# A memory-augmented recurrent transformer block: attention masks by multiplication, an earlier start, and a feed-forward part scheduled into the same ordered program

## The chip, the cores and the metric

One core of a Trainium2 chip runs the whole program. The metric is device time in microseconds (us), median of several runs. The core has five engines that run side by side, each in the order of its own instruction stream: TensorE (PE, matrix products from SBUF into PSUM), VectorE (DVE), ScalarE (ACT), GpSimd (POOL) and SyncE (SP, here only a queue of DMA issues). DMAs are issued from SP, ACT and POOL.

## The reference

The input x has 2048 tokens of width 640. It is normalised (layernorm without scale and shift) and cut into 64 segments of 32 tokens. Each segment is put behind a memory of 8 rows, attention runs over these 40 rows with 32 heads of width 128, and the first 8 rows of the projected output are the next segment's memory; the other 32 are the segment's result. So the 64 segments form a chain that can't be run in parallel. Then a feed-forward part (FFN) with a squared ReLU, 640 to 1728 to 640, is added to the residual.

```python
mask = (idx[:, None] < M) | (idx[:, None] >= idx[None, :])
for s in range(n_seg):
    h = jnp.concatenate([mem, xs], axis=1)
    q, k, v = (jnp.einsum('btd,dhe->bhte', h, W) for W in (Wq, Wk, Wv))
    scores = jnp.where(mask, jnp.einsum('bhqe,bhke->bhqk', q, k) * scale, -1e9)
    o = jnp.einsum('bhte,hed->btd', jnp.einsum('bhqk,bhke->bhqe', _softmax(scores), v), Wo)
    mem, out_s = o[:, :M], o[:, M:]
h = x + attention(layernorm(x))
h2 = h + relu(layernorm(h) @ w1 + b1)**2 @ w2 + b2
```

Memory queries see all 40 rows; a token sees the memory and the tokens up to itself.

## The kernel before, in words

**Blocks and steps.** 128 tokens are a block, four segments; there are 16 blocks (b) and 64 steps (b, sp). A step takes 32 rows through the chain: 8 memory rows and the first 24 tokens of the segment. The last 8 tokens of the four segments of a block are a tail of 32 rows, whose q, k and v are computed once a block by `tail_pass_fill`, and whose output projection by `wo_tail_fill`. These are cut into units and put in the list `fill`; `run_fill` (L228) pops some of them at places in a step where PE would wait. 32 rows fill a quarter of the PE array, so four groups of heads stand side by side (G = 4), in partitions 32g to 32g+31.

**Order.** A hand-written order holds on PE, ACT, DVE and POOL within the attention part (`manual_schedule`, L142): each of these runs its instructions as the program text emits them. SP's issues are placed by the framework. The FFN lies behind it, in pools of its own.

**A step** (`main_step`, L320): q in two halves, each 20 matmuls of 512 columns into a PSUM tile of tag mm (two buffers), copied out by ACT and DVE (`half`, `evac`); then the previous step's token values (`token_values`, L299: for each head index four matmuls with the step's values and four with the tail's); then k, v and transposes of q and k. The scores pss (L348) begin with two matmuls of the identity with mask tiles, which write 0 or -30000, and 64 matmuls of keys and queries add to them. ACT takes exp in three pieces: p for the memory queries, pk_s and p_lz for the token queries. p is spread over the groups (pbd), summed (pz), inverted and broadcast through PE (rz, rd, pb, rs), and gives the memory rows' values po, which are scaled into oT. For the token queries the sums are pzk (L406), their inverses rk, spread by POOL into rb. The output projection pw (`wo_pass`, L288) is 128 matmuls; in its middle `norm` (L421) turns rb by PE into pr and DVE makes pnk and pnl, the weights for the next step's token values. Then o is copied out by DVE, stored to DRAM (o_main), and `mem_to_hT` (L275) turns its 8 memory rows into hT, which the next step's q waits for.

**Layernorm** (L105): statistics on DVE, the inverse root on POOL as eleven or so small instructions (L117 to L127), the normalisation on DVE. Block b+1's statistics run at the start of block b, its normalisation and its five transposes (`ln_transpose`) at the start of the second step. x tiles have one buffer, and the next one's load is issued on SP.

**Start.** x of block 0, the memory, then Wq, Wk, Wv (for each, four slices of 128 partitions and 1 MB, and four of 32 partitions and 256 KB) and Wo (four of 1.25 MB) are issued, alternating between SP and ACT. x of block 1 comes after them. All three tail passes of block 0 run before the first step.

**FFN** (L474): when the attention's pools are released, w1, w2, b1 and b2 are loaded. Four tiles of 512 tokens: for each of four blocks the rows of o and x are loaded (main and tail rows apart, so that a block takes 13 DMAs), added, normalised, transposed into hnT; hb is the residual plus b2 (POOL, L518). Then 14 groups of 5 matmuls (psf, L525), each followed by ReLU on ACT and a square on DVE (f1T, one buffer), and for each block two groups of 14 matmuls (psy, L538), whose result plus hb is yo, stored by 8 DMAs per block.

Of the kernel before, what the change touches and what calls it, by code (L numbers as in the profile page):

```python
# [9 lines left out]
ALU = mybir.AluOpType  # L10
AX = mybir.AxisListType
F32 = mybir.dt.float32
# [5 lines left out]
def kernel(  # L18
# [16 lines left out]
    nc = tc.nc  # L35
# [21 lines left out]
    NEG = -30000.0  # L57
# [23 lines left out]
    for g in range(G):  # L81
# [3 lines left out]
    nc.vector.memset(mask_m[0:32], 0.0)  # L85
    nc.gpsimd.affine_select(out=mask_m[0:32], in_=mask_m[0:32], compare_op=ALU.is_ge,
                            fill=NEG, base=M, pattern=[[0, HG], [1, HD]], channel_multiplier=-1)
    mask_t = const.tile([128, 4, HG, M + TL], BF16)
    nc.vector.memset(mask_t[0:32], 0.0)
    for sp in range(4):  # L90
        mt = mask_t[0:32, sp]
        nc.gpsimd.affine_select(out=mt, in_=mt, compare_op=ALU.is_ge, fill=NEG, base=-TL * sp,
                                pattern=[[0, HG], [0, M + TL]], channel_multiplier=1)
        nc.gpsimd.affine_select(out=mt, in_=mt, compare_op=ALU.is_ge, fill=NEG, base=TL * sp + TL - 1,
                                pattern=[[0, HG], [0, M + TL]], channel_multiplier=-1)
        mtt = mask_t[0:32, sp, :, M:M + TL]
        nc.gpsimd.affine_select(out=mtt, in_=mtt, compare_op=ALU.is_ge, fill=NEG, base=TL * sp,
                                pattern=[[0, HG], [1, TL]], channel_multiplier=-1)
    for g in range(1, G):
        nc.gpsimd.dma_start(out=mask_m[32 * g:32 * g + 32], in_=mask_m[0:32])  # L100
        nc.gpsimd.dma_start(out=mask_t[32 * g:32 * g + 32], in_=mask_t[0:32])
    ones64 = const.tile([64, 128], BF16)
    nc.vector.memset(ones64[:], 1.0)

    def layernorm(pool, src, dst, strips=False):  # L105
        FMAX = nc.vector.BN_STATS_FMAX
        nsub = 1
        while D // nsub > FMAX or D % nsub:
            nsub += 1
        st = pool.tile([128, nsub, nc.vector.BN_STATS_DIM], F32, tag="lnst")  # L110
        xr = src.rearrange("p (s f) -> p s f", s=nsub)
        for s_ in range(nsub):
            nc.vector.bn_stats(out=st[:, s_, :], in_=xr[:, s_, :])
        mv = pool.tile([128, nc.vector.BN_AGGR_DIM], F32, tag="lnmv")
        nc.vector.bn_aggr(out=mv[:], in_=st[:])
        ve = pool.tile([128, 1], F32, tag="lnve")
        nc.gpsimd.tensor_scalar(out=ve[:], in0=mv[:, 1:2], scalar1=EPS, scalar2=None, op0=ALU.add)  # L117
# [462 lines left out]
```

## Time and profile before

| what | us |
|---|---|
| median of 5 runs (1438.25 to 1443.64) | 1442.44 |
| the profiled execution's own time | 1442.44 |
| its span, first to last instruction | 1440.7 |
| PE busy | 1233.6 (86%) |
| DVE busy | 508.8 (35%) |
| ACT busy | 465.8 (32%) |
| POOL busy | 194.2 (13%) |

The profile is one execution, recorded by the hardware. A row of its timeline gives the start, the duration, the engine (PE for matmuls, PEld for their weight loads, SPq and ACTq for issues of DMAs), the line of the kernel, the operation, output<-inputs with shapes, and the count; in brackets stands the idle time before it and what ended that. A group row gives the busy time of all, the mean ns of one, and the idle time before them. A row of the windows view gives, for a stretch, the busy time of PE, PEld, DVE, ACT and POOL, PE's granted clock, the DMA engines' busy share and GB/s. A row of the waits view gives the total, the number and the longest of a wait.

### The profile page before, as it was taken

What the parts mean: (1) busy time and instruction counts of PE and PEld (TensorE: products, weight loads), DVE (VectorE), ACT (ScalarE), POOL (GpSimd) and SP (SyncE); (2) the same over time, 40 slices, a digit from 0 to 9 for tenths busy, and PEclk for the clock granted to TensorE, in tenths of its full rate; (3) what the DMA queues carried; (4) which work ended last, traced back from release to release, by engine and by line L of the source; (5) the groups of instructions that cost most, each with busy time, mean ns of one, the idle gap of its engine ahead of it and who ended that gap; (6) DMA issues with size and microseconds to landing.
All of it is one profiled execution on the core that took longest, in us unless ns stands there. A gap on an engine that the chain in (4) does not pass through costs nothing.

```text
span 1440.7 us, 69707 instructions
## 1 busy us (share of the span) xinstructions
PE 1233.6 (86%) x32376; PEld 705.3 (49%) x32376; DVE 508.8 (35%) x1398; ACT 465.8 (32%) x1001; POOL 194.2 (13%) x684
## 2 busy tenths in 40 slices
PE   1399999999999999989999999998999998158888
PEld 0155555555555555555555555554555555024444
DVE  1033334333333333433333333333434333144442
ACT  0233333333333333333333333333333333022222
POOL 2001010101010100001010101010101000263420
PEclk9899999999999999999999999999999999569999
DMA  9800000000000000000000000000000000521200
GB/s 312 285 10 5 12 6 12 6 12 6 12 6 12 6 12 5 13 6 12 6 12 5 12 5 13 6 10 6 12 5 8 5 7 8 162 47 48 53 26 19
DMA packets 39396, 44.00 MB, mean 31 GB/s; under 512 B 24448, under 2 KB 36464, under 8 KB 37184
## 3 DMA queue, kind: packets, MB, share of 16 engines
q1 hardware_dynamic: 29440, 23.25, 5.8%
q10 hardware_dynamic: 9344, 15.98, 3.5%
q8 instruction: 253, 4.15, 1.2%
q0 software_dynamic: 320, 0.30, 0.1%
q14 instruction: 39, 0.32, 0.1%
HBM read 33.44 MB, written 5.94 MB: 27 GB/s over the span
## 4 chain that ended last, share of the span: by engine, by line
PE 77%; DMA 7%; DVE 5%; ACT 5%; issue 3%; POOL 1%; ACTq 0%; DVEq 0%; SPq 0%
PE ps L198 38%; PE pw L218 11%; PE pt L211 6%; PE psy L538 5%; PE psf L525 4%; PE ps L218 3%; ACT row L191 2%; DMA xt<-in_A_x_dram 2%; PE po L393 2%; DVE row L193 2%; PE po L304 1%; PE pss L361 1%; PE pss L357 1%; DMA wk<-in_A_Wk_dram 1%; DMA w<-in_B_w_dram 1%
## 5 line engine op out<-in xcount | busy, mean ns | idle before, releaser
L198 PEld LDWEIGHTS <-hT 128*32 128x32 bf16 x7680 | 179.7, 96 | 211.8 <-issue 54.7
L191 ACT CAST row<-ps 128x512 bf16<-128x512 f32 x192 | 112.8, 588 | 327.9 <-PE ps L198 313.4
L198 PE MATMUL ps<-wv,hT 128*32 128x512 bf16 x2560 | 177.3, 383 | 15.5 <-DVE vr L193 12.0
L218 PE MATMUL pw<-wo,oT 128*32 128x160 bf16 x8320 | 172.4, 234 | 17.7 <-issue 10.5
L198 PE MATMUL ps<-wk,hT 128*32 128x512 bf16 x2560 | 162.7, 383 | 16.8 <-DVE row L193 11.5
L218 PEld LDWEIGHTS <-oT 128*32 128x32 bf16 x8320 | 148.6, 97 | 40.8 <-issue 21.3
L198 PE MATMUL ps<-wq,hT 128*32 128x512 bf16 x2560 | 153.8, 382 | 14.4 <-ACT row L191 11.3
L193 DVE CAST row<-ps 128x512 bf16<-128x512 f32 x128 | 88.5, 692 | 211.2 <-PE ps L198 211.2
L211 PE MATMUL pt<-ident,row 128*128 128x128 bf16 x1280 | 113.4, 221 | 38.6 <-ACT row L191 26.2
L211 PEld LDWEIGHTS <-row 128*128 128x128 bf16 x1280 | 76.0, 98 | 129.5 <-issue 98.6
L416 POOL CAST rb<-rk 128x256 bf16<-128x256 f32 x64 | 25.8, 403 | 565.7 <-DVE rk L414 565.7
L191 ACT COPY kT<-pt 128x512 bf16<-128x512 bf16 x128 | 75.4, 589 | 17.4 <-PE pt L211 17.3
L380 DVE TENSOR_TENSOR pbd<-p,ones 128x256 bf16<-128x256 bf16 x128 | 48.7, 422 | 90.3 <-ACT p L364 90.3
L193 DVE CAST vr<-ps 128x512 bf16<-128x512 f32 x64 | 44.3, 692 | 101.5 <-PE ps L198 101.5
L525 PE MATMUL psf<-hnT,w 128*128 128x512 bf16 (+1 forms) x280 | 71.8, 419 | 9.5 <-ACT r L528 6.4
L314 POOL COPY oTt<-oT 128x256 bf16<-128x256 bf16 x64 | 25.8, 403 | 392.2 <-DVE oT L193 385.4
L191 ACT CAST oT<-po 128x256 bf16<-128x256 f32 x128 | 41.4, 376 | 92.4 <-PE po L308 91.0
L191 ACT COPY qT<-pt 128x512 bf16<-128x512 bf16 x64 | 37.6, 587 | 98.0 <-PE pt L211 98.0
L538 PE MATMUL psy<-w,f1T 128*128 128x320 bf16 x448 | 68.0, 300 | 0.3 <-DVE f1T L529 0.2
L426 DVE TENSOR_TENSOR pnk<-pk_s,pr 128x256 bf16<-128x256 bf16 x64 | 27.0, 421 | 116.1 <-PE pr L424 116.1
L404 DVE TENSOR_TENSOR oT<-po,rs 128x128 bf16<-128x128 f32 x128 | 31.3, 287 | 74.4 <-ACT rs L400 74.4
L198 PEld LDWEIGHTS <-hTt 128*32 128x32 bf16 x1920 | 41.8, 97 | 29.9 <-issue 9.8
(104 smaller groups left out, 1509.7 us busy)
## 6 DMA issues: line engine op xcount, KB each, us to landing
o_main<-o SPq DMA_DIRECT2D x65, 40.0 KB
xt<-in_A_x_dram SPq DMA_DIRECT2D x16, 160.0 KB
wo<-in_A_Wo_dram SPq DMA_DIRECT2D x2, 1280.0 KB
wo<-in_A_Wo_dram ACTq DMA_DIRECT2D x2, 1280.0 KB
w<-in_B_w_dram SPq DMA_DIRECT2D x1, 2160.0 KB
w<-in_B_w_dram ACTq DMA_DIRECT2D x1, 2080.0 KB
wq<-in_A_Wq_dram ACTq DMA_DIRECT2D x2, 1024.0 KB
wq<-in_A_Wq_dram SPq DMA_DIRECT2D x2, 1024.0 KB
```

The costliest lines, as they stand in the source:

```text
L191: nc.scalar.copy(out=out_, in_=in_)
L193: nc.vector.tensor_copy(out=out_, in_=in_)
L198: nc.tensor.matmul(ps[32 * g:32 * g + 32, :], lhsT=lhs(c), rhs=w[:, c, g * EG + n * 512:g * EG + (n + 1) * 512], start=(c == 0), stop=(c = ...
L211: nc.tensor.transpose(out=pt[:, k * 128:(k + 1) * 128], in_=row[:, i * 128:(i + 1) * 128], identity=ident[:])
L218: nc.tensor.matmul(ps[32 * g:32 * g + 32, 0:DG], lhsT=lhs(h), rhs=wo[:, h, g * DG:(g + 1) * DG], start=(h == 0), stop=(h == H - 1))
L314: nc.gpsimd.tensor_copy(out=oTt[:, :, sp * TL:(sp + 1) * TL], in_=oT[:, :, SEG:NQ])
L380: nc.vector.tensor_tensor(out=pbd[:, a], in0=p[:, a].unsqueeze(2).to_broadcast([128, HG, G, M]), in1=ones4[:].unsqueeze(1).unsqueeze(3).to ...
L393: nc.tensor.matmul(po[:, i * SEG:(i + 1) * SEG], lhsT=v[:, i * E:(i + 1) * E], rhs=pbd[:, a, i].rearrange("p g q -> p (g q)"), start=(a == ...
L404: nc.vector.tensor_tensor(out=oT[:, k * 16:(k + 1) * 16, 0:M].rearrange("p (g i) q -> p g i q", g=2), in0=pov[:, gs], in1=rs[:].rearrange( ...
L426: nc.vector.tensor_tensor(out=pnk[:], in0=pk_s[:], in1=pr[:, 0:NK], op=ALU.mult)
L525: nc.tensor.matmul(ps[0:fs, :], lhsT=w1[:, c, fc * 128:fc * 128 + fs], rhs=hnT[:, c, :], start=(c == 0), stop=(c == DC - 1))
L538: nc.tensor.matmul(ps[:, 0:320], lhsT=f1T[0:fs, fc, k * 128:(k + 1) * 128], rhs=w2[0:fs, fc, cs], start=(fc == 0), stop=(fc == FC - 1))
```

## The change: what it does

**Masks.** The mask matmuls go. The mask tiles now hold 1 and 0; POOL multiplies pk_s (its first 24 columns of each head) and p_lz by them after exp. For the memory queries' tail keys, a table ones4t (made once) takes the place of ones4. The first key-query matmuls start the PSUM tile.

**Token sums.** pzk, rk and rb move from behind pb into the middle of the output projection (`sums`), and pr, pnk and pnl from there behind it. The token-value matmuls are the same, all of the step's values first and then all of the tail's.

**Layernorm** is cut in three: first half of the statistics; second half and root; normalisation. For block b+2 these run in the middle of the projections of steps (b, 2), (b, 3) and (b+1, 0). x tiles have two buffers. The transposes stay at the second step of a block; the tail copy goes first.

**Start.** x of blocks 0 and 1 is loaded first and both layernorms run before the first step. The wide weight slices are all on SP, the narrow ones all on ACT, Wo on both. The tail passes of block 0 run inside the first step, each before the main pass of its weight.

**FFN** comes into the same ordered program and the same pools. w1 is loaded by five SP DMAs in the last step, into the slot of Wq; w2 by POOL's queue after the first tile's root. Its working tiles lie in the slots of Wk, Wv and Wo. The rows are loaded for whole tiles of four blocks (9 DMAs a block, in natural order), the next tile's ahead: its statistics run in the groups of psf, its root (one for four blocks) and hb on POOL after them, its normalisation and transposes between the groups of psy. f1T and hnT have two buffers, r has three, psy uses the four psum_v tiles, and yo is stored by one DMA per block.

```diff
-            nc.tensor.matmul(psv[:, :, M:SEG], lhsT=ident[:], rhs=mask_m[:], start=True, stop=False,
-                             skip_group_check=True)
-            nc.tensor.matmul(psv[:, :, NQ:NC], lhsT=ident[:], rhs=mask_t[:, sp], start=False, stop=False,
-                             skip_group_check=True)
...
+            pkh = pk_s[:].rearrange("p (i q) -> p i q", q=SEG)[:, :, 0:HD]
+            nc.gpsimd.tensor_tensor(out=pkh, in0=pkh, in1=mask_m[:], op=ALU.mult)
+            nc.gpsimd.tensor_tensor(out=p_lz[:, :, HD:SEG], in0=p_lz[:, :, HD:SEG], in1=mask_t[:, sp], op=ALU.mult)
...
-            def norm():
-                pr = psum_t.tile([128, 512], F32, tag="pt", name="pr")
+            def sums():
+                pzk = psum_t.tile([128, 512], F32, tag="pt", name="pzk")
...
+                for f in side.get((b, sp), ()):
+                    f()
+            o = wo_pass(b * 4 + sp, sums)
+            pr = psum_t.tile([128, 512], F32, tag="pt", name="pr")
...
+                if sp == 2 and b + 2 < NB:
+                    lns = ln_block(b + 2)
+                    side[b, 2], side[b, 3], side[b + 1, 0] = [lns[0]], [lns[1]], [lns[2]]
+                if b == NB - 1 and sp == 3:
+                    last = ffn_load
...
+        load_x(1)
...
-                (nc.sync if c % 2 else nc.scalar).dma_start(out=w[:, c, :], in_=w2d[c * DG:c * DG + 128, :])
+                nc.sync.dma_start(out=w[:, c, :], in_=w2d[c * DG:c * DG + 128, :])
             for g in range(G):
-                (nc.sync if g % 2 else nc.scalar).dma_start(out=w[32 * g:32 * g + DR, 4, :],
-                                                            in_=w2d[g * DG + 128:(g + 1) * DG, :])
+                nc.scalar.dma_start(out=w[32 * g:32 * g + DR, 4, :], in_=w2d[g * DG + 128:(g + 1) * DG, :])
```

The ends of attention and the FFN's loop:

```diff
+        loads(0)
+        token_values(*pend.pop())
...
+        for k in range(NK4):
+            stats(0, k)
+        root(0)
+        ffn_load2()
+        loads(1)
+        for k in range(NK4):
+            apply(0, k)
+            turn_f(0, k, "act" if k % 2 == 0 else "dve")
...
+                if nxt and fc in (2, 4, 6, 8):
+                    stats(t + 1, fc // 2 - 1)
+                if t == 0 and fc >= FC - NK4:
+                    hbias(nc.vector, 0, fc - FC + NK4)
+            if nxt:
+                root(t + 1)
+            if t + 2 < NTL:
+                loads(t + 2)
...
+                    if nxt and k in (1, 2):
+                        apply(t + 1, (k - 1) * 2 + hf)
+                    nc.vector.tensor_tensor(out=yo[:, cs], in0=ps[:, 0:320], in1=hbs[t % 2 * NK4 + k][:, cs], op=ALU.add)
+                    if nxt and k in (1, 2):
+                        turn_f(t + 1, (k - 1) * 2 + hf)
+                nc.sync.dma_start(out=out2d[b * 128:(b + 1) * 128, :], in_=yo)
```

`loads`, `stats`, `root`, `apply`, `turn_f` and `hbias` are new functions of the FFN: a tile's row loads, residual sum and statistics, inverse root, normalisation, transposes, and residual plus b2.

More of the change, by code (lines that the diff above doesn't have):

```diff
@@ L334, in main_step @@
                 token_values(*pend.pop())
+            if first:
+                fill.extend(first[1])
+                run_fill(100)
             half(wk, lhs, 0, kr, "act")
@@ L339, in main_step @@
             turn(kr, 0, kT[:, 0:4], "act")
+            if first:
+                fill.extend(first[2])
+                run_fill(100)
+            if last:
+                last()
             pv0 = psum.tile([128, 512], F32, tag="mm", name="ps")
```

332 lines of the change are left out of this document (191 added, 141 removed).

## The prediction, made before the change was run

> **What bounds the kernel now.** I read the page first: span, the slices, the chain that ended last.
>
> ```profile
> span 1440.7 us, 69707 instructions
> ...
> PE   1399999999999999989999999998999998158888
> ...
> PE 77%; DMA 7%; DVE 5%; ACT 5%; issue 3%; POOL 1%; ACTq 0%; DVEq 0%; SPq 0%
> ```
>
> Each digit is one fortieth of the span (36 us). TensorE (PE) is full in the middle, the 64 recurrent steps, and empty at two places: the first two slices (loading) and slices 34 and 35 (from attention to FFN). So there are three stages, with three limits. The profiled execution took 1442.44 us, which is also the median of the five runs; its span is 1440.7, so 1.7 us lie around the span. All sums below are on the span's clock.
>
> **Start.** The windows view gives DMA GB/s in its last column; the timeline gives start, duration, engine, line.
>
> ```profile
> 23.00:30.00 7.00, 1.14 (x12) 0.18 (x4) 0.00 (x0) 0.00 (x0) 0.00 (x0) 1.00 1.03 414
> 30.00:34.00 4.00, 0.00 (x0) 0.00 (x0) 0.00 (x0) 0.00 (x0) 0.00 (x0) 1.00 1.04 221
> 66.00:68.00 2.00, 0.00 (x0) 0.00 (x0) 0.00 (x0) 0.00 (x0) 0.00 (x0) 0.50 0.07 22
> ...
> 68.27 0.89 DVE L113 BATCH_NORM_STATS2 st<-xt 128x6 f32<-128x320 bf16 x2 [52.99 <-DMA xt<-in_A_x_dram]
> ...
> 70.00 2.33 PE L198 MATMUL ps<-wk,hT 128*32 128x512 bf16 x20 [8.28 <-DVE row L193]
> ...
> 73.23 1.42 PE L198 MATMUL ps<-wv,hT 128*32 128x512 bf16 x12
> ...
> 82.97 0.19 PE L277 MATMUL pm<-ident,o 128*128 128x32 bf16 x1 [0.43 <-DVE o L223]
> ```
>
> The weights have landed by 66 us (22 GB/s after it), and yet the first step hands its memory on (pm) at 82.97: VectorE (DVE), in program order, sat on the statistics of block 1, whose x was loaded last, so that PE waited 8.28 us for a copy queued behind them. The change loads both x blocks first and finishes both layernorms, which removes that 8.28 us wait; gives ACT the twelve 256 KB slices and half of Wo; and runs the q, k and v tail passes each when its own weight is there. What is late next are the transfers themselves, 21.5 MB before and after. Wide slices move at 414 GB/s, 32-partition slices at 221. Ahead of the last Wv slice lie 12.9 MB wide (31 us) and 3.15 MB narrow (14 us), with 2 us to start: 47 us; with ACT's 2.6 MB of Wo (wide) drawn ahead, 53. From Wv's arrival, the v tail pass (half of the 40-matmul rate above, 2.3 us) and then 82.97-73.23 = 9.7 us lead to pm: 59 to 65. But pm also needs all of Wo, landed at 66 as before, half a projection (1.3) and its copy (0.7): 68. I take 68: **15 us gained**. Bounds: with the transfers ending 6 us later because one queue carries more of them (no row shows that), 9; with narrow and wide slices mixing well and ending at 62, 19.
>
> **Loop.** A steady step with a tail pass as filler:
>
> ```profile
> 600.24 0.26 PE L350 MATMUL pss<-mask_m,ident 128*128 128x192 bf16 x1
> ...
> 600.48 0.37 PE L357 MATMUL pss<-qT,kTt 128*32 128x16 bf16 x32
> ...
> 602.10 0.39 ACT L370 ACTIVATE pk_s<-pss 128x256 bf16<-128x256 f32 x1
> ...
> 602.46 0.42 DVE L386 TENSOR_TENSOR rd<-ident,rz 64x256 bf16<-64x256 bf16 x1
> ...
> 603.23 0.18 PE L409 MATMUL pzk<-ones,pk_s 128*128 128x4 bf16 x1
> ...
> 603.41 1.05 PE L198 MATMUL ps<-wq,hTt 128*32 128x512 bf16 x16
> ...
> 605.94 0.28 PE L424 MATMUL pr<-ident,rb 128*128 128x128 bf16 x2
> 606.15 1.29 PE L218 MATMUL pw<-wo,oT 128*32 128x160 bf16 x64
> 606.26 0.42 DVE L426 TENSOR_TENSOR pnk<-pk_s,pr 128x256 bf16<-128x256 bf16 x1 [1.86 <-PE pr L424]
> 606.60 0.21 DVE L427 TENSOR_TENSOR pnl<-p_lz,pr 128x64 bf16<-128x64 bf16 x1
> ...
> 607.21 0.18 PEld L198 LDWEIGHTS <-hTt 128*32 128x32 bf16 x8
> ...
> 607.50 0.33 DVE L223 CAST o<-pw 128x160 bf16<-128x160 f32 x1 [0.68 <-PE pw L218]
> ...
> 608.24 0.20 DVE L281 CAST hT<-pm 128x40 bf16<-128x40 f32 x1 [0.42 <-PE pm L279]
> ...
> 608.49 2.34 PE L198 MATMUL ps<-wq,hT 128*32 128x512 bf16 x40
> ```
>
> PE works in order, so differences of neighbouring starts are what its groups cost. **Masks:** two matmuls go, 600.48-600.24 = 0.24 us, on a stretch where PE has no gap. **pzk** leaves the place ahead of the filler (603.41-603.23 = 0.18) for the middle of the output projection, where pr stood (606.15-605.94 = 0.21): 0.21 gained there and in the middle, of which pr is given back behind the projection. **The tail of the step:** call 607.21 T, the end of the projection. Before, o is copied by T+0.62, pm follows, hT is written from T+1.03 and q starts at T+1.28. After, pr (0.21) and two fill units stand ahead of pm, which moves to T+0.67 at the earliest, its result usable at about T+1.03; DVE must do o, then pnk and pnl (spacing 0.34, then 0.18) before hT: 0.62+0.34+0.18 = T+1.15. So q at T+1.40, 0.12 later. Net 0.24+0.18+0.03-0.12 = 0.33 us a step. **Layernorm:** the normalisation of the next block moves from right ahead of its transposes into an earlier projection:
>
> ```profile
> PE pt L180 <- DVE xn L136: 22.1, 16, 12.7
> ```
>
> Of the 22.1 us, 12.7 is the first block; (22.1-12.7)/15 = 0.63 a block goes. That step has a second o copy (0.33) now behind pnl, so I keep 0.35 of it. Per block 4 x 0.33 + 0.35 = 1.7; fifteen blocks and a last one without fillers (0.15 a step): **26 us gained**.
>
> The masks are now GpSimd (POOL) multiplications of 192 and 64 columns, which before doesn't show. The nearest rows:
>
> ```profile
> L518 POOL TENSOR_TENSOR hb<-ht,b2b 128x640 f32<-128x640 bf16 x16 | 22.6, 1415 | 60.9 <-DVE ht L508 60.9
> ...
> 1379.95 0.43 DVE L529 TENSOR_TENSOR f1T<-r 128x512 bf16<-128x512 bf16 x1 [0.65 <-ACT r L528]
> ...
> 1380.89 1.40 POOL L518 TENSOR_TENSOR hb<-ht,b2b 128x640 f32<-128x640 bf16 x1 [0.47 <-DVE ht L508]
> ...
> 1381.26 1.31 DVE L529 TENSOR_TENSOR f1T<-r 64x512 bf16<-64x512 bf16 x1
> ```
>
> At 1415/640 = 2.2 ns a column they take 0.43 + 0.15, from 602.55 (exp done at 602.49) to 603.2; pzk reads them at 605.5. The cover is 2.3 us: nothing on the path. Behind them on POOL wait only rb, which needs pzk anyway, and the copies into oTt and qT for the next step, several us from use; and on DVE nothing but hT waits behind pnk, which is counted above. Bounds: nothing, to the whole 0.6 a step if something else waits for POOL. That can happen: a DVE multiplication that takes 0.43 alone took 1.31 while POOL's 1.40 us one ran. rd (602.46) starts 0.09 ahead of POOL's first multiplication, so I expect POOL to wait and nothing to be lost; if POOL wins, rd is 0.4 late, pb behind it stalls PE by as much, and 64 steps give back 26 us. The Trainium skill ("SBUF — State Buffer", section "SBUF: two separate sides") says that the shared port pair is an exclusive lock, that whoever starts first has it for the whole instruction, and that DVE needs it when it has two SBUF inputs. The 1.31 us row agrees; by that rule the sum holds if rd's lead holds, and is the next rival if not.
>
> The reordered token-value matmuls are the same 64, and the DVE statistics in mid-projection (0.9 us at most, against a 1.29 us half) are covered; without cover each costs its length once a block.
>
> **FFN.**
>
> ```profile
> 1230.00 0.45 PE L218 MATMUL ps<-wo,oTt 128*32 128x160 bf16 x13 [1.62 <-issue]
> ...
> 1250.58 0.49 DVE L508 TENSOR_TENSOR ht<-ot,xt 128x640 bf16<-128x640 bf16 x1 [10.21 <-DMA xt<-in_A_x_dram]
> ...
> 1252.03 0.21 DVE L115 BATCH_NORM_AGGREGATE mv<-st 128x2 f32<-128x12 f32 x1
> ...
> 1256.45 0.45 DVE L136 TENSOR_SCALAR hn<-ht,mv,rstd 128x640 bf16<-128x640 bf16 x1 [4.22 <-POOL rstd L127]
> ...
> 1277.15 12.64 PE L525 MATMUL psf<-hnT,w 128*128 128x512 bf16 x45 [0.78 <-ACT hnT L515]
> ...
> 1398.83 0.45 PE L513 MATMUL pt<-ident,hn 128*128 128x128 bf16 x5 [0.69 <-DVE hn L136]
> ...
> 1402.13 17.07 PE L525 MATMUL psf<-hnT,w 128*128 128x512 bf16 x70 [0.78 <-ACT hnT L515]
> ...
> 1419.14 16.96 PE L538 MATMUL psy<-w,f1T 128*128 128x320 bf16 x112
> ...
> L499 SPq DMA_DIRECT2D ot<-o_main x64: 290/322/576, 1231.5 to 1363.3; - x64
> ```
>
> Before, 46.7 us pass between the last projection (1230.45) and the first FFN matmul (1277.15): weights and rows are only then loaded, and four layernorms run one after another, each with its 4.2 us of POOL. After, w1 and the rows of tile 0 are issued within the last step into freed weight slots. What is left: 1 us because pnk and pnl are now behind the last projection with nothing to cover them (1231.5), o's copy, four statistics of 1252.24-1250.58 = 1.66 us, one root for all four (4.2), then four normalisations, transposes and copies overlapping (about 5): 1231.9+6.6+4.2+5 = 1247.7. **29.5 us gained.** It hangs on tile 0's 36 row loads: SP issues one in 0.32 us (median, last row) to 0.58, so all in 12 to 21. They can start once the last Wv pass frees its slot, 607.21-600.48 = 6.7 us ahead of the end of a projection, and the two final projections take 256 matmuls at 64 in 1.3, with their pause 7 us: 14 of cover, and statistics that follow one block at a time. Just in time; without any cover some 16 us come on top.
>
> From there on before took 1440.7-1277.15 = 163.5 us, its first three tiles (1402.13-1277.15)/3 = 41.7 each, the last, with no layernorm beside it, 17.0+17.0 = 34.0. After, the next tile's layernorm and transposes stand within the tile: 34.0 x 4 plus 20 transposes (4 x 0.45) three times, 141.4, and an end of 4 (one store for eight): 145.4. **18 us gained.** DVE has 1.66 more in every second 1.08 us group, so it falls up to 2.5 us behind, which the three r buffers just hold. w2 (2.1 MB) comes on POOL's queue after the root, issued at 1243 and needed at 1264.5; its cost is nothing if it lands within 21 us. POOL's queue landed 160 KB in 6.7 us, and 0.1 KB in 7.5:
>
> ```profile
> b2b<-in_B_b_dram POOLq DMA_DIRECT2D x1, 160.0 KB, 6.7
> b1b<-in_B_b_dram POOLq DMA_DIRECT2D x1, 0.1 KB, 7.5
> ```
>
> So size does not show, and 7.5 plus 2.1 MB at 221 GB/s is 17. Bounded by 13 times the 160 KB row it would be 90, 70 too late; I take the first.
>
> **Sum:** 1440.7-15-26-29.5-18 = 1352.2, and 1.7 around it: **1354 us**.
>
> **The rivals.** (1) POOL wins the port and rd waits: the loop gives back 26 us, 1380. For it: only 0.09 us of lead. Against: rd needs only DVE's order, while POOL's start needs exp, whose end (602.49) lies behind rd's start. (2) A late transfer in the FFN: out stores queue on SP behind the 36 row loads of the tile after next (16 us), the two yo buffers stay full, DVE's normalisation waits, and PE stalls some 4 us in two tiles; or w2 lands late: 1362. (3) The loop yields the masks only (0.24 x 64 = 15) because the DVE tail is longer than read: 1365. (4) The change doesn't do what it says, the early loads wait for their slots until attention ends: the 29.5 us stay, 1383. (5) Slower: POOL's multiplications are so slow on their strided 192 columns that pzk waits. They have 2.9 us from 602.55 to 605.5; the gains outside are 88 us, 1.4 a step, so above 4.3 us, seven times my price, the kernel is slower; at 5 us, (5-2.9) x 64 = 134 is added: 1488. The 2.2 ns a column speaks against it. (6) Still faster, under 1337: transfers mix well and the steps lose further waits.
>
> **Numbers.** Forecast 0.55 (its own range 1337 to 1368, from the bounds of the start and 0.15 us a step either way), rival 1 0.14, rival 2 0.11, rival 3 0.08, rival 4 0.04, rival 5 0.02, rival 6 0.06. The range 1337 to 1381 leaves out rivals 4 to 6. About 0.3% (4.3 us) is what a measurement can tell from no change. Only rival 5 is not faster, and a mixture of several losses could end at no change: faster 0.96, same 0.02, slower 0.02.
>
> **What would show it.** The first pm near 68; starts of exp p in neighbouring steps 0.3 us closer; POOL's multiplication over before 603.5 in the step's clock and rd still 0.42 long; the first psf some 16 us after the last projection; tiles of 34 to 36 us with PE unbroken. Wrong if rd grows to 0.8, if PE waits for pzk, or if psy or the FFN transposes wait for a DMA.

## The result and the profile after

| what | before | after |
|---|---|---|
| median, us | 1442.66 (16 runs, 1438.25 to 1449.58) | 1347.52 (9 runs, 1344.43 to 1353.26) |
| ratio to before | | 0.9339, 95% interval 0.9322 to 0.9357 |
| span of the profiled execution | 1440.7 | 1345.9 |
| first step's pm | 82.97 | 71.86 |
| first pm to last pm | 1121.8 | 1095.0 |
| last pm to the end of the final projections | 25.7 | 24.2 |
| from there to the first psf | 46.7 | 18.3 |
| first psf to the end | 163.5 | 136.6 |

The kernel is 95 us faster. The forecast was 1354, 6.5 us above the measurement, inside its range. The five stages of the table gain 11.1 + 26.8 + 1.5 + 28.4 + 26.9 = 94.7 us of span; forecast were 15, 26, nothing, 29.5 and 18.

From the page of the changed kernel, the span, PE's slices and the shares of the chain that ended last:

```profile
span 1345.9 us, 69184 instructions
...
PE   1699989898989899999999999989898989849999
...
PE 82%; DVE 5%; DMA 5%; ACT 5%; issue 3%; SPq 1%; POOL 0%; ACTq 0%; DVEq 0%
```

The second slice went from 3 to 6, the hole of two slices between attention and FFN (1 and 5) is now one slice (4), and the last four slices are full. PE's share of the chain rose from 77% to 82%.

**The start**, PE's timeline of the changed kernel (start, duration, engine, line, operation; in brackets the idle time before it and what ended that):

```profile
56.20 0.40 PE L206 MATMUL ps<-wv,hTt 128*32 128x512 bf16 x4 [0.92 <-DMA wv<-in_A_Wv_dram]
59.23 3.18 PE L206 MATMUL ps<-wv,hTt 128*32 128x512 bf16 x28 [2.63 <-DMA wv<-in_A_Wv_dram]
...
68.72 1.29 PE L226 MATMUL pw<-wo,oT 128*32 128x160 bf16 x64 [0.79 <-DVE oT L438]
...
71.86 0.19 PE L285 MATMUL pm<-ident,o 128*128 128x32 bf16 x1 [0.22 <-DVE o L231]
```

The wait for a copy behind the second block's statistics is gone, and in its place PE waits for Wv's last slice. From 59.23 to pm it takes 12.6 us: 2.9 for the last 28 matmuls of the v tail pass, to 62.17, at a granted clock of 0.50 (windows view, 57.4 to 64.1), and 9.7 from there, as forecast.

**A step** of the changed kernel, the same place as in the prediction, all engines:

```profile
223.64 0.42 DVE L420 TENSOR_TENSOR rd<-ident,rz 64x256 bf16<-64x256 bf16 x1
...
223.75 0.72 POOL L404 TENSOR_TENSOR pk_s<-pk_s,mask_m 128x192 bf16<-128x192 bf16 x1 [6.12 <-ACT pk_s L400]
...
224.43 0.30 POOL L405 TENSOR_TENSOR p_lz<-p_lz,mask_t 128x64 bf16<-128x64 bf16 x1
...
226.94 0.18 PE L450 MATMUL pzk<-ones,pk_s 128*128 128x4 bf16 x1
...
228.34 0.29 PE L463 MATMUL pr<-ident,rb 128*128 128x128 bf16 x2
228.46 0.33 DVE L231 CAST o<-pw 128x160 bf16<-128x160 f32 x1 [0.95 <-PE pw L226]
...
229.47 0.20 DVE L289 CAST hT<-pm 128x40 bf16<-128x40 f32 x1 [0.18 <-PE pm L287]
```

rd starts 0.11 us ahead of POOL's multiplication and takes 0.42 us as before. The multiplications take 1.0 us, not the 0.58 of the forecast, and end at 224.73, 2.2 us before pzk reads them. Over all 64 steps rd takes 416 to 419 ns.

**The FFN**, PE's timeline of the changed kernel:

```profile
1209.31 16.24 PE L621 MATMUL psf<-fk,fw 128*128 128x512 bf16 x70 [0.68 <-DVE b1f L613]
1225.48 6.40 PE L642 MATMUL psy<-fw,fk 128*128 128x320 bf16 x42
1231.81 0.45 PE L591 MATMUL pt<-ident,fw 128*128 128x128 bf16 x5
1232.10 2.17 PE L642 MATMUL psy<-fw,fk 128*128 128x320 bf16 x14
...
1243.55 15.40 PE L621 MATMUL psf<-fk,fw 128*128 128x512 bf16 x70
...
1325.56 16.96 PE L642 MATMUL psy<-fw,fk 128*128 128x320 bf16 x112
```

No psf or psy after the first waits for anything: tiles start at 1209.31, 1243.55, 1276.89 and 1310.23, so they are 34.2, 33.3 and 33.3 us long, against 41.7 before.

### The profile page after: what moved, and what is told of

The parts are those of the page before. It is cut to its first block, busy times and chain, and to the rows that moved or that the text cites. A ratio compares the mean times of both kernels' runs of the same rounds, so it can differ in the third digit from the quotient of the medians.

```text
span 1345.9 us, 69184 instructions
## 1 busy us (share of the span) xinstructions
PE 1206.6 (90%) x32248; PEld 703.1 (52%) x32248; DVE 507.6 (38%) x1406; ACT 465.2 (35%) x999; POOL 224.0 (17%) x643
## 4 chain that ended last, share of the span: by engine, by line
PE 82%; DVE 5%; DMA 5%; ACT 5%; issue 3%; SPq 1%; POOL 0%; ACTq 0%; DVEq 0%
PE ps L206 41%; PE pw L226 12%; PE pt L219 6%; PE psy L642 5%; PE psf L621 5%; PE ps L226 3%; ACT row L199 3%; PE po L427 2%; DVE row L201 2%; DMA wq<-in_A_Wq_dram 2%; PE pss L391 1%; DMA wk<-in_A_Wk_dram 1%; PE po L312 1%; PE pss L387 1%; PE po L318 1%
## 5 line engine op out<-in xcount | busy, mean ns | idle before, releaser
L226 PEld LDWEIGHTS <-oT 128*32 128x32 bf16 x8320 | 149.1, 98 | 37.6 <-issue 17.4
L404 POOL TENSOR_TENSOR pk_s<-pk_s,mask_m 128x192 bf16<-128x192 bf16 x64 | 45.9, 718 | 446.6 <-ACT pk_s L400 446.6
L642 PE MATMUL psy<-fw,fk 128*128 128x320 bf16 x448 | 68.5, 300 | 0.0
L621 PE MATMUL psf<-fk,fw 128*128 128x512 bf16 (+1 forms) x280 | 62.4, 383 | 0.7 <-DVE b1f L613 0.7
L206 PE MATMUL ps<-wq,hTt 128*32 128x512 bf16 x640 | 48.2, 396 | 13.5 <-DMA wq<-in_A_Wq_dram 8.2
L206 PE MATMUL ps<-wk,hTt 128*32 128x512 bf16 x640 | 51.2, 397 | 9.1 <-DMA wk<-in_A_Wk_dram 8.6
```

What stands on the lines that cost most here:

```text
L206: nc.tensor.matmul(ps[32 * g:32 * g + 32, :], lhsT=lhs(c), rhs=w[:, c, g * EG + n * 512:g * EG + (n + 1) * 512], start=(c == 0), stop=(c = ...
L226: nc.tensor.matmul(ps[32 * g:32 * g + 32, 0:DG], lhsT=lhs(h), rhs=wo[:, h, g * DG:(g + 1) * DG], start=(h == 0), stop=(h == H - 1))
L404: nc.gpsimd.tensor_tensor(out=pkh, in0=pkh, in1=mask_m[:], op=ALU.mult)
L621: nc.tensor.matmul(ps[0:fs, :], lhsT=w1[:, c, fc * 128:fc * 128 + fs], rhs=hnT[:, c, :], start=(c == 0), stop=(c == DC - 1))
L642: nc.tensor.matmul(ps[:, 0:320], lhsT=f1T[0:fs, fc, k * 128:(k + 1) * 128], rhs=w2[0:fs, fc, cs], start=(fc == 0), stop=(fc == FC - 1))
```

## The experiments

Each is the changed kernel with one edit; the last takes two of them together. The ratio is to the kernel before, which ran on the same chip in turn with each; "after" is 0.9339 (0.9322 to 0.9357). For the loop I use a second reading, worked out from the timeline: the distance between the starts of exp p in neighbouring steps, median over blocks 1 to 14, for the four steps of a block.

| kernel | median, us | ratio, 95% | steps 0-1, 1-2, 2-3, 3-0 |
|---|---|---|---|
| before | | | 18.42, 16.66, 19.97, 17.45 |
| after | 1347.52 | 0.9339 (0.9322 to 0.9357) | 17.43, 16.38, 19.67, 17.04 |
| masks by PE | 1364.94 | 0.9463 (0.9441 to 0.9484) | 17.73, 16.68, 19.98, 17.35 |
| sums back | 1352.30 | 0.9374 (0.9352 to 0.9397) | 17.39, 16.69, 19.63, 17.11 |
| layernorm back | 1356.64 | 0.9407 (0.9384 to 0.9431) | 18.09, 16.38, 19.67, 17.04 |
| token values in pairs | 1344.97 | 0.9329 (0.9305 to 0.9352) | 17.37, 16.38, 19.68, 17.04 |
| POOL three times | 1346.04 | 0.9331 (0.9311 to 0.9350) | 17.55, 16.38, 19.67, 17.04 |
| queues alternating | 1349.14 | 0.9337 (0.9319 to 0.9356) | |
| Wo on SP | 1347.16 | 0.9332 (0.9308 to 0.9356) | |
| one narrow DMA | 1382.79 | 0.9571 (0.9550 to 0.9591) | |
| filler in the last block | 1348.34 | 0.9334 (0.9317 to 0.9351) | |
| two r buffers | 1345.05 | 0.9324 (0.9302 to 0.9346) | |
| rows early | 1340.21 | 0.9287 (0.9267 to 0.9308) | |
| rows early, Wo on SP | 1341.36 | 0.9300 (0.9278 to 0.9322) | |

**Masks by PE again.**

```diff
+            nc.tensor.matmul(psv[:, :, M:SEG], lhsT=ident[:], rhs=mask_m[:], start=True, stop=False,
+                             skip_group_check=True)
+            nc.tensor.matmul(psv[:, :, NQ + M:NC], lhsT=ident[:], rhs=mask_t[:, sp], start=False, stop=False,
+                             skip_group_check=True)
...
-            nc.gpsimd.tensor_tensor(out=pkh, in0=pkh, in1=mask_m[:], op=ALU.mult)
-            nc.gpsimd.tensor_tensor(out=p_lz[:, :, HD:SEG], in0=p_lz[:, :, HD:SEG], in1=mask_t[:, sp], op=ALU.mult)
```

> The changed kernel with its token masks added by two identity matmuls of 192 and 64 columns again, and without the POOL multiplications (the memory queries keep ones4t). Theory: on a stretch where PE has no gap each step gets longer by the two starts that were 0.24 us apart before, a little less since the second matmul has 64 columns instead of 128; 0.2 x 64 = 13 us, 1360 us. Rival A, PE waits elsewhere in the step and takes the two matmuls for nothing: 1347 to 1350. Rival B, the POOL multiplications hold up DVE or PE somewhere: no slower than 1347, and rd or pnk shorter than in the changed kernel.

17.4 us slower, 0.30 us in every step; more than the 0.2 expected. The same stretch of one step in PE's timeline, first this kernel:

```profile
221.76 1.26 PE L207 MATMUL ps<-wv,hT 128*32 128x512 bf16 x20
222.96 0.26 PE L385 MATMUL pss<-mask_m,ident 128*128 128x192 bf16 x1
223.05 0.19 PE L387 MATMUL pss<-mask_t,ident 128*128 128x64 bf16 x1
223.17 0.37 PE L392 MATMUL pss<-qT,kTt 128*32 128x16 bf16 x32
```

then the changed kernel:

```profile
220.56 1.26 PE L206 MATMUL ps<-wv,hT 128*32 128x512 bf16 x20
221.65 0.40 PE L387 MATMUL pss<-qT,kTt 128*32 128x16 bf16 x32
```

The two masks' own starts lie 0.21 us ahead of the keys' (223.17 - 222.96). But the 20 matmuls of Wv in front of them also take 1.20 us to the next start, where the keys follow them after 1.09. So a group that is removed takes 0.11 us at the border with its neighbour along with it, and its price by neighbouring starts was too low: 0.32 here. The Trainium skill ("TensorEngine Tiling (Array Packing)", section "Key Properties") says that a change of the tiling mode drains TensorE: the masks are full-array matmuls among tiled ones, and the 0.11 us agrees. The runs don't separate this from the full-array weight load that stands there too. Rival A and rival B both fall.

**Sums back to their old place.**

```diff
+            pzk = psum_t.tile([128, 512], F32, tag="pt", name="pzk")
...
+            nc.gpsimd.tensor_copy(out=rb[:], in_=rk[:].unsqueeze(2).to_broadcast([128, 2 * G, SEG]))
             run_fill(F2)
...
-            o = wo_pass(b * 4 + sp, sums)
+            o = wo_pass(b * 4 + sp, norm)
```

> The changed kernel with pzk, rk and rb ahead of the second group of fillers again, and pr, pnk and pnl in the middle of the output projection. Theory: the move was worth 0.09 us a step (0.18 + 0.03 gained, 0.12 lost at the tail), so 6 us come back: 1353. In the last block the four pzk matmuls stand again in PE's gap ahead of the projection; if that gap (0.84 us instead of 0.66) is what halves the granted clock there, its projections take 1.3 + 1.3 us again instead of 1.6 + 2.3 and 3 us of the 6 are given back: 1350. Rival, the longer DVE tail cost more than the middle gained: 1340 or less.

4.8 us slower by the medians, as the theory said, though the intervals overlap. The steps put the loss at one place: 0.31 us between the second and the third step and nearly nothing at the other three, 0.30 a block, where the forecast had 0.09 in each. The timeline of that place in block 5 shows why (PEld are PE's weight loads):

```profile
436.45 0.30 POOL L405 TENSOR_TENSOR p_lz<-p_lz,mask_t 128x64 bf16<-128x64 bf16 x1
436.54 0.10 PEld L444 LDWEIGHTS <-pk_s 128*128 128x128 bf16 x1 [0.24 <-POOL pk_s L404]
...
436.80 0.10 PEld L446 LDWEIGHTS <-p_lz 128*128 128x128 bf16 x1 [0.17 <-POOL p_lz L405]
```

At its old place pzk comes so early in this step that PE waits for both of POOL's multiplications: from pb's start to the next group of matmuls it needs 0.75 us (median of blocks 1 to 14), in the changed kernel 0.21, and pzk then 0.19 in the middle of the projection. The kernel before had no such multiplications. So the total came out right by luck: what the move spares is a wait that the POOL masks would have caused, not the 0.09 a step of the theory. In the last block one of the two slow projections was at full clock again (below).

**Layernorm back.**

```diff
+                        if b + 1 < NB:
+                            lns = ln_block(b + 1)
+                            lns[0]()
+                            lns[1]()
...
                     if sp == 1:
+                        if b > 0:
+                            lns[2]()
...
-                    side[b, 2], side[b, 3], side[b + 1, 0] = [lns[0]], [lns[1]], [lns[2]]
```

> The changed kernel with the layernorm of block b+1 at its old places in the loop: both halves of the statistics at the start of block b, the normalisation right ahead of the transposes of the second step. Theory as predicted: 0.35 us a block come back, 5 us, 1353. From the trace, where the first step of a block got 0.98 us shorter and the other three 0.28 to 0.41: 0.65 us a block, 10 us, 1357. Rival, the first step got shorter by something else: 1347.

9.1 us slower, all of it in the first step of a block: 0.66 us, the whole 0.63 that the waits view of before showed. In this kernel's waits view (total, times, longest) PE's wait is back; the longest, 15.3, is the start's:

```profile
PE pt L188 <- DVE xn L139: 25.4, 15, 15.3
```

(25.4 - 15.3)/14 = 0.72 us a block. The 0.28 us that the prediction took off for the second o copy behind pnl was not there.

**Token values in pairs.**

```diff
-            for i in range(HG):
                 for g in range(G):
                     r = slice(32 * g, 32 * g + 32)
                     nc.tensor.matmul(po[g][:, i * SEG + HD:(i + 1) * SEG], lhsT=vt[r, i * E:(i + 1) * E],
```

> The changed kernel with the token-value matmuls in the old order, four of the step's values and four of the tail's in turn. Theory: the same 64 matmuls, nothing: 1347.5 within 2. Rival, the new order is part of the 0.3 us that each step gained: at 0.1 us a step 1354.

No difference: the steps are the same within 0.06 us, and the interval lies across that of the changed kernel.

**POOL's multiplications three times.**

```diff
+            for _ in range(3):
+                nc.gpsimd.tensor_tensor(out=pkh, in0=pkh, in1=mask_m[:], op=ALU.mult)
+                nc.gpsimd.tensor_tensor(out=p_lz[:, :, HD:SEG], in0=p_lz[:, :, HD:SEG], in1=mask_t[:, sp], op=ALU.mult)
```

> The changed kernel with POOL's two mask multiplications done three times in a row (the masks hold 0 and 1, so the result is the same). One pair takes 0.72 + 0.30 us, of which 0.3 is the wait for rd; two more pairs add about 1.4 us, and pzk comes 2.2 us after the end of the first. Theory, they lie beside other work on POOL: 1347.5 within 3. Rival A, their time is on the path: 1.4 x 64 = 90 us, 1437. Rival B, they hold up DVE's operations that run meanwhile (rd, oT) by some 0.4 us a step: 1373.

The same time. Timeline of one step of this kernel:

```profile
223.80 0.42 DVE L421 TENSOR_TENSOR rd<-ident,rz 64x256 bf16<-64x256 bf16 x1
...
223.91 0.72 POOL L405 TENSOR_TENSOR pk_s<-pk_s,mask_m 128x192 bf16<-128x192 bf16 x1 [6.12 <-ACT pk_s L400]
...
224.85 0.55 POOL L405 TENSOR_TENSOR pk_s<-pk_s,mask_m 128x192 bf16<-128x192 bf16 x1
...
226.13 0.31 POOL L406 TENSOR_TENSOR p_lz<-p_lz,mask_t 128x64 bf16<-128x64 bf16 x1
...
227.09 0.18 PE L451 MATMUL pzk<-ones,pk_s 128*128 128x4 bf16 x1
```

All six end at 226.44 and pzk comes at 227.09: the 2.2 us of cover (from 224.89, the end of the first pair) are real, and 1.5 of them could be filled for nothing. The wide multiplication takes 0.72 beside rd and 0.55 where rd is over, so it is POOL that gives way; rd stays at 0.42.

**Weight slices alternating between SP and ACT.**

```diff
-                nc.sync.dma_start(out=w[:, c, :], in_=w2d[c * DG:c * DG + 128, :])
+                (nc.sync if c % 2 else nc.scalar).dma_start(out=w[:, c, :], in_=w2d[c * DG:c * DG + 128, :])
             for g in range(G):
-                nc.scalar.dma_start(out=w[32 * g:32 * g + DR, 4, :], in_=w2d[g * DG + 128:(g + 1) * DG, :])
+                (nc.sync if g % 2 else nc.scalar).dma_start(out=w[32 * g:32 * g + DR, 4, :],
+                                                            in_=w2d[g * DG + 128:(g + 1) * DG, :])
```

> The changed kernel with the weight slices alternating between SP and ACT again, as before (x first, tail passes inside the first step). In the changed kernel the last Wv slice arrives at 59.2 us and starts the chain that ends in pm at 71.9. Theory: that is late because ACT's queue runs all narrow slices in the first 33 us, where only 250 GB/s are moved, and then draws 2.6 MB of Wo ahead of Wv; with both queues in weight order Wv arrives at about 52 and the end of Wo (66) sets pm, at 68: 1343.5. Rival, the rate of the transfers as a whole is the limit, and the order of the queues moves nothing: 1347.5. Rival, ACT sits on its issues of wide slices and its copies for the q tail pass come late: 1350 or more.

The same time (1349.14), and the first step's pm at 73.33, 1.5 us later; in the nine kernels whose start is that of the changed one it lies anywhere from 69.2 to 72.3. PE never waits for Wv in this kernel, so Wv did come sooner. But ACT's timeline shows what the third expectation said:

```profile
42.27 5.88 ACTq L175 DMA_DIRECT2D wo<-in_A_Wo_dram  x2
48.19 1.28 ACT L200 ACT_TABLE_LOAD   x1 [48.19 <-DMA wv<-in_A_Wv_dram]
49.48 1.07 ACT L200 CAST row<-ps 128x512 bf16<-128x512 f32 x2
```

ACT is done with its issues at 48.15, and only then copies the q tail pass; in the changed kernel its first copy stands at 33.28. Giving ACT only the small slices is what lets the tail passes start; it costs Wv's arrival.

**Wo on SP alone.**

```diff
-            (nc.sync if j % 2 else nc.scalar).dma_start(out=wo[:, j * 8:(j + 1) * 8, :], in_=wov[:, j * 8:(j + 1) * 8, :])
+            nc.sync.dma_start(out=wo[:, j * 8:(j + 1) * 8, :], in_=wov[:, j * 8:(j + 1) * 8, :])
```

> The changed kernel with all four slices of Wo on SP's queue, behind Wv, and ACT's queue left with the narrow slices alone. Theory: the 2.6 MB of Wo that ACT's queue draws ahead of Wv (6.3 us at 414 GB/s) are why the last Wv slice arrives at 59 instead of 53; without them Wv arrives near 53, the end of all transfers (66) sets the first step's pm, at 68 instead of 71.9 (the 68 of the prediction): 1343.6. Rival, Wv arrives no sooner, since the rate of the first 33 us is what delays it: 1347.5; or Wo, now all behind Wv, lands later than 66 and gives the gain back.

PE's timeline:

```profile
54.77 1.70 PE L206 MATMUL ps<-wv,hTt 128*32 128x512 bf16 x28 [0.90 <-DMA wv<-in_A_Wv_dram]
...
69.33 1.26 PE L226 MATMUL pw<-wo,oT 128*32 128x160 bf16 x32 [2.82 <-DMA wo<-in_A_Wo_dram]
```

Wv comes 4.5 us sooner, as expected, but now Wo's last slice is late, at 69.3, and pm stands at 71.02; the time is the same. So two limits lie close together: the chain from Wv, and the end of all transfers, which is at 69 and not at 66 as before. The last clause of the rival holds.

**One narrow DMA per weight.**

```diff
-            for g in range(G):
-                nc.scalar.dma_start(out=w[32 * g:32 * g + DR, 4, :], in_=w2d[g * DG + 128:(g + 1) * DG, :])
+            nc.scalar.dma_start(out=w[:, 4, :], in_=w2d.rearrange("(g q) e -> g q e", q=DG)[:, 128:DG, :])
```

> The changed kernel with the four 32-partition slices of each weight loaded by one DMA of 128 partitions and 1 MB. Theory: the narrow slices cost by the partitions that they reach; as wide ones they move at the 414 GB/s of the wide slices, all 21.5 MB land by 54 us instead of 66, Wv by about 46, and the first step's pm comes near 59 instead of 71.9: 1335. Rival, each narrow slice costs by its 8 KB rows, wherever they go: no gain, 1347.

Both expectations are wrong: 35 us slower. The windows view of this kernel (last two columns: share of the 16 DMA engines that was busy, GB/s):

```profile
10.00:20.00 10.00, 0.71 (x5) 0.45 (x5) 0.64 (x2) 0.00 (x0) 3.21 (x15) 1.00 0.26 93
```

The share is a quarter, as if four of the sixteen engines carried these DMAs, whose source has an outer dimension of 4; the trace does not name the engines. The Trainium skill ("DMA: Bandwidth & Descriptors", section "Why a DMA increments its semaphore by 16 and not by 1") says that a DMA is spread over the largest number of engines, up to 16, that divides the slowest dimension of both patterns; by that rule it would be four here, and the 0.26 agrees. Whether narrow slices would be cheaper as true 128-partition transfers stays open.

**A filler in the last block.**

```diff
             run_fill(F2)
+            if b == NB - 1:
+                pd = psum.tile([128, 512], F32, tag="mm", name="pd")
+                for c in range(3):
+                    for g in range(G):
+                        nc.tensor.matmul(pd[32 * g:32 * g + 32, :], lhsT=hT4[:, c, sp, :],
+                                         rhs=wv[:, c, g * EG:g * EG + 512], start=True, stop=True)
```

> The changed kernel with twelve more matmuls of 512 columns (0.8 us, result unused) in PE's gap ahead of the projection in the four steps of the last block. Theory: the granted clock falls to 0.50 in three of these projections because PE stands idle there for 0.84 us; with the gap closed the projection halves take 1.3 us each instead of 1.6 and 2.3, steps 61 to 63 get 1.2 us shorter each, 1344. Rival, the clock falls for the load before it, whatever the gap: 1347.5 or a little more.

In this run the last two distances between exp p, from step 61 to 63, were 15.66 and 15.63 us instead of 17.06 twice. But with queues alternating they were 15.62 twice, without a filler and with the same gap of 0.84 us, and so they were with rows early and Wo on SP. So the test is inconclusive; the time did not move either.

**Two r buffers in the FFN.**

```diff
-                r = rs_[fc % 3]
+                r = rs_[fc % 2]
```

> The changed kernel with two r buffers in the FFN, as before, instead of three. Theory of the prediction: the statistics of the next tile (1.6 us on DVE in every second group of 1.08 us) make DVE fall behind, and only the third buffer hides it; with two, ACT and then PE wait some 0.6 us at each of the four places of three tiles: 1355. Rival, the gain of the FFN's tiles is the clock alone (17.1 us of psf before, with its first matmuls at half clock, 15.4 after), and the buffers do nothing: 1347.5.

The same time. First psf to end grows from 136.6 to 137.8, all of it in the first tile, whose psf takes 17.53 us instead of 16.24. The windows view shows the granted clock (third column from the end) at the start of that tile, first this kernel, then the changed one:

```profile
1207.00:1211.30 4.30, 4.08 (x10) 1.51 (x12) 0.43 (x1) 0.69 (x1) 0.00 (x0) 0.50 0.99 322
1209.30:1211.10 1.80, 1.79 (x5) 0.69 (x6) 0.00 (x0) 0.00 (x0) 0.00 (x0) 0.51 1.02 369
```

The half clock lasts 4.4 us into this kernel's tile and 1.8 into the other's; half of the difference is 1.3 us, the whole growth. PE waits for an r buffer in no tile, and psf of the other tiles is 15.40 with two buffers as with three. The rival holds.

**Rows early.** o_main and o_tail lie in natural row order, so that the rows of four blocks take 9 DMAs instead of 36; tile 0's go into Wq's slot.

```diff
+                nc.sync.dma_start(out=ots[r0:r0 + HD, :].rearrange("r (k d) -> r k d", d=D),
+                                  in_=o_main[b * 4 + sp + 1:b * 4 + sp + 14:4].rearrange("k r d -> r k d")[M:SEG])
...
                 nc.sync.dma_start(out=w1v[:, c, :], in_=B_w1[c * 128:(c + 1) * 128, :])
+            rows0()
+            side[NB - 1, 3] = [lambda: stats(0, 0)]
...
-        loads(0)
         token_values(*pend.pop())
+        for k in (1, 2):
+            stats(0, k)
...
+        stats(0, 3)
+        root(0)
```

> The changed kernel with o_main and o_tail in natural row order, so that the rows of a tile take 9 DMAs instead of 36; tile 0's rows go into free space of Wq's slot and are issued right behind w1, and its statistics run one block in the last step, two during the last token values' projection, one behind it. Theory: between the last projection and the first psf (18.3 us) stand only statistics, root, normalisation and transposes, bounded by DVE and by the loads' arrival; with the statistics done at 1191 the root ends at 1195.5 and psf starts near 1199 instead of 1209: 1337. Rival A, the statistics delay the last step's chain by as much as they save: 1347. Rival B, the rows still come late (w1 ahead of them on SP): 1342 to 1347.

7 us faster than the changed kernel, and the intervals do not overlap. Less than expected, because the rows came later than thought. (The profiled execution took 1345.55, well above this kernel's median, so its trace accounts for only 2 of the 7 us: 4.4 gained from the last pm to psf, 1.7 lost behind it.) DVE's timeline:

```profile
1186.93 0.49 DVE L366 TENSOR_TENSOR fw<-fw 128x640 bf16<-128x640 bf16 x1 [4.39 <-DMA fw<-o_tail]
...
1188.50 0.27 DVE L231 CAST o<-pw 128x160 bf16<-128x160 f32 x1
```

The first statistics stand in the last step and wait 4.39 us for their rows; the copy of o, behind them in DVE's order, waits with them.

**Rows early and Wo on SP**, with the first three statistics behind the last token values (Wo's lines as above; this cut is against the kernel with rows early):

```diff
-            side[NB - 1, 3] = [lambda: stats(0, 0)]
...
-        for k in (1, 2):
+        for k in range(3):
             stats(0, k)
```

> Rows in natural order and loaded early, Wo on SP, and the three first statistics of tile 0 behind the last token values' copies instead of one in the last step, where it waited 4.4 us for its rows and held up the last projection's copy. Theory: the last step's chain is undisturbed, the root ends at about 15 us behind the last step's pnk, psf starts 3 us sooner than with the rows alone, and Wo's place gives up to 3.9: 1334. Rival, the rows are late in any place and nothing is gained on the 1340 of the rows alone.

psf starts at 1198.61, 10.7 us earlier than in the changed kernel; 3.9 of these lie ahead of the last pm, 2.2 in the start and the rest in the loop. From the last pm to psf it is 35.6 us, against 38.0 with the rows alone and 42.4 in the changed kernel. The median is still that of the rows alone. DVE's timeline shows one part of what is lost behind psf:

```profile
1207.29 0.49 DVE L365 TENSOR_TENSOR fo<-fo 128x640 bf16<-128x640 bf16 x1 [1.73 <-DMA fo<-o_tail]
```

Now tile 1's rows are late within tile 0. DVE waits for them, ACT finds no free r buffer, and PE has gaps of 0.29 and 0.65 us. First psf to end grows to 139.5, from 136.6; 1.5 of these 2.9 us are the half clock, which lasts 4.8 us into tile 0 here. With the rows alone it is 138.3, with a wait of 1.8 us for the same rows.

## Why the prediction was right, point by point

**Start: 15 forecast, 11.1 measured; mechanism right, size off.** PE's 8.28 us wait went, and the transfers were late next, as said. The mis-sized term is the landing of Wv and Wo: Wv at 47 to 53 was forecast and 59.2 measured, Wo at 66 and 69 measured (with Wo on SP). Of the 59.2, Wo's two slices on ACT's queue are 4.5 us (54.77 with Wo on SP), where the forecast had 6. For the rest the page's GB/s row points at the rate: the first slice of the span moved 251 GB/s, where it moved 312 before and 314 with the queues alternating again. All the narrow slices then run at the head, on ACT's queue. The 2.3 and 9.7 us from Wv to pm were 2.9 and 9.7. The stated bound for "one queue carries more of them", 9, was the nearer one. The order of the queues can't mend it: both other orders gave the same time.

**Loop: 26 forecast, 26.8 measured; the number is luck, four errors that cancel.** Masks were put at 0.24 us a step; undoing them cost 0.30 (0.11 of it at the border with the Wv group, which neighbouring starts don't show). Layernorm was put at 0.35 a block; undoing it cost 0.66. These two give 1.22 + 0.66 = 1.88 us a block, and the loop as a whole shows 1.98. So about 0.1 a block is left for the move of the sums, which was put at 0.36: the tail of the step gives back nearly all that the move gains. The 0.30 that undoing the move cost is a wait for POOL's masks, which the kernel before could not have. Against the gain stands a loss in the last block that no term had: its last two distances are 17.06 us against 15.98 before, at half the granted clock in the projection.

**POOL: nothing on the path, and so it was.** The price, 0.43 + 0.15, was too low: 0.72 + 0.30, of which 0.17 is the wait for rd. The cover of 2.3 us was right (2.2). The rival that cost 26 us needed POOL to win the port; rd kept its lead (0.11 us in the step shown) and its 0.42 us in every step. That POOL waits for rd is what the rule quoted in the prediction from the Trainium skill ("SBUF — State Buffer", section "SBUF: two separate sides") says; the trace agrees on who waits, and shows 0.17 us of it.

**FFN start: 29.5 forecast, 28.4 measured.** The chain of statistics, one root, normalisations and transposes is what stands between, but the rows of tile 0 were not quite in time: the SP queue issued the last at 1197.09, 6 us behind the last projection (1191.04), and DVE waited for them ahead of three of the four statistics. From the waits view, 1190 to 1202 (total, times, longest):

```profile
DVE fv L561 <- DMA fv<-o_tail: 2.3, 3, 1.4
```

These 2.3 us are on the path, since the root waits for the last statistics; the other steps took about a microsecond less than their price. Loading them earlier alone was worth 4.4 us there by the time from the last pm to psf (42.4 to 38.0).

**FFN: 18 forecast, 26.9 measured; mechanism right, size off.** The tiles were put at 34.0 + 1.8 and came out at 33.3. Two terms were too dear. The 34.0 came from the last tile before, whose 70 psf took 17.07 us; the windows view of before shows the granted clock there in PE's column (third from the end):

```profile
1402.00:1407.00 5.00, 4.87 (x15) 1.86 (x15) 0.47 (x2) 1.46 (x3) 0.00 (x0) 0.66 0.02 6
1407.00:1412.00 5.00, 5.00 (x24) 2.24 (x23) 2.08 (x5) 3.18 (x5) 0.00 (x0) 1.00 0.00 0
```

That tile began after a pause of PE, at 0.66; a tile that follows another without a pause has 15.40. This is 1.7 us a tile. And five transposes were priced by their 0.45 us duration, where neighbouring starts (1231.81 to 1232.10) give 0.29: 0.6 us a tile. The end, from the issue of the last store (1343.07), took 2.8 us instead of 4. That it takes three r buffers to hold what DVE falls behind was wrong: with two, PE waited in no tile either.

**The other rivals.** Of the late transfer in the FFN the first half happened, once, in tile 0. DVE's timeline:

```profile
1238.15 0.49 DVE L646 TENSOR_TENSOR fv<-psy,fv 128x320 bf16<-128x320 f32 x1 [2.97 <-DMA out_dram<-fv]
```

DVE waited 2.97 us for a yo buffer whose store stood on SP behind row loads (issued at 1236.21, between them), but PE had no gap. Rows that came late within tile 0 stopped PE only when the start was moved ahead, for 0.9 us in all. Early loads waiting for their slots, and POOL too slow by seven times, did not happen.

## What to carry to other kernels

A group's price by the distance to the next start leaves out what it does to the group in front of it, so compare the same stretch with and without it. A duration taken from a stage that begins after a pause carries the low clock of that pause; look at the granted clock of the row before it is multiplied. When a wait is removed, ask of each candidate that comes next how far behind it is: here Wv's chain and the end of the transfers lay so close together that mending one alone gained nothing. And when an edit is undone, ask whether it now meets something else that is new: the sums at their old place waited for the new masks.

## What was not expected of the hardware

The granted clock in the last block. Its last three steps have no fillers, and in the changed kernel their output projection falls to half clock. PE's timeline:

```profile
1145.36 1.58 PE L226 MATMUL pw<-wo,oT 128*32 128x160 bf16 x64 [0.84 <-DVE oT L438]
...
1147.07 2.33 PE L226 MATMUL pw<-wo,oT 128*32 128x160 bf16 x64
```

and the windows view of the same kernel ahead of it, in the middle of it and as a whole:

```profile
1142.80:1146.20 3.40, 2.12 (x71) 1.70 (x71) 1.75 (x6) 1.43 (x5) 0.98 (x2) 1.00 0.01 2
1146.50:1147.00 0.50, 0.50 (x20) 0.25 (x8) 0.00 (x0) 0.00 (x0) 0.00 (x0) 0.50 0.12 33
1146.20:1149.60 3.40, 3.40 (x98) 2.74 (x86) 0.36 (x2) 0.00 (x0) 0.74 (x2) 0.50 0.02 5
```

The same 64 matmuls take 1.29 us at full clock. The low stretch lasts 3.4 us (1146.2 to 1149.6), and no single gap of PE in that step is longer than 0.84 us; but in the 3.4 us ahead of it the gaps add up to 1.3 us. The next two low stretches begin at 1163.3 and 1180.3, each 17.1 us after the one before, which is five times 3.4, and PE is again busy for 2.12 of the 3.4 us ahead of them. So a step that is held to 17.06 us by the low clock brings the next one to the same place; that this keeps the steps slow is argued, not tested.

Each kernel was profiled once, and they differ. Of the twelve kernels with an edit, both of the last two distances are long in six, one in three, and none in three. The kernel before shows a low stretch in its last step's projection (1217.9 to 1221.3) and once in the middle of the loop (955.1 to 958.5), with PE busy for 1.74 of the 3.4 us ahead of that. PE's busy share alone does not decide: with queues alternating, 2.14 of 3.4 us (1161.4 to 1164.8) brought no fall, and with the sums back 2.52 (1160.3 to 1163.7) did.

The Trainium skill ("TensorE: Matmul & The Clock Gate", section "Part 1: The HAM clock gate (the "warmup" mystery)") tells of a free-running window of 3.4 us over which PE's activity is judged, and of an idle window that lowers the clock. The length of the low stretches and their distances agree with that; that gaps of under a microsecond can lower it, added up, is what these runs show with a number. What decides in the end was not found out.
